# Two attention layers in one kernel: the other layer first, and the output projection in seven Strassen products, half of them between the dense heads

## The chip, the cores and the metric

The kernel runs on one core of a Trainium2 chip. The metric is the device time of one execution in microseconds, shown as the median of several runs. The engines that matter are TensorE (PE, with its weight load PEld), VectorE (DVE), ScalarE (ACT) and GpSimd (POOL). Transfers between DRAM and the core's SBUF are issued from the queues of SP (the sync engine), ACT and POOL. Each engine works through its own queue in order; semaphores hold an instruction until what it needs is there.

## The reference

Two attention layers run on inputs of their own, and their outputs are concatenated. Each has 2048 positions, 1024 features and 32 heads of 32.

```python
def _A_ref(x, wqkv, wo):
    ...
    W, dil = 8, 2
    ...
    idx = pos[:, None] - off[None, :]
    ...
    logits = jnp.einsum("bhsd,bhswd->bhsw", q, kg) * scale
    logits = jnp.where(mask[None, None, :, :], logits, -1e9)
    attn = _softmax(logits, axis=-1)
    o = jnp.einsum("bhsw,bhswd->bhsd", attn, vg)
    return (lambda x, *d: x.transpose(*d))(o, 0, 2, 1, 3).reshape(B, S, D) @ wo

def _B_ref(x, wqkv, wo):
    ...
    mask = (idx[:, None] - idx[None, :] >= 0) & (idx[:, None] - idx[None, :] < W)
    scores = jnp.where(mask[None, None], scores, -1e9)
    p = _softmax(scores, axis=-1)
    o = jnp.einsum("bhqk,bhkd->bhqd", p, v)
    return (lambda x, *d: x.transpose(*d))(o, 0, 2, 1, 3).reshape(B, S, D) @ wo
```

In layer A (the window layer here) each position attends to eight positions, two apart. In layer B (the dense layer here) it attends to the 256 positions that end with itself. Both end with an output projection, a 2048 x 1024 by 1024 x 1024 product.

## The kernel before

The work is cut into eight *units*: four chunks of 512 positions of each layer. `ORDER` puts the four dense units first, then the four window units. A unit has eight *groups* of four heads (128 features). For each group `qk_items` computes q and k: two matrix products, each eight feature blocks (k) of three 128x512 matmuls (L518). There are three matmuls because every operand is kept as a high and a low part: `Stream.parts` casts the loaded fp32 data to fp32r (the high part, L201 on ACT or L204 on DVE, whichever a model of the engines says ends first) and subtracts (the low part, L207 on DVE), and `TERMS` multiplies high by high, high by low and low by high. `v_items` computes v for four or two groups at a time (L583). `o_items(u, n)` computes one 128-row block of a unit's output projection (L645): eight groups' outputs `ot`, also high and low (`finish`, L822 and L826), times eight blocks of `wo`, summed in one PSUM bank, copied out (`copy_out`, L536 or L539) and stored (L662).

All weights and inputs come through one list, `items`, in the order in which they are used. `Stream.load_to` issues a load of 512 KB per item on POOL's queue (L159) into a ring of `NRAW` = 3 raw tiles; `split_to` splits it into the tiles of `wpool` (3 buffers) or `xpool` (`NX`). A raw tile is loaded again only when its last subtraction is done.

The order of the program is written by a loop at the end of the kernel. It keeps a clock for each engine (`Clock`) and takes, at each step, the next thing that is ready from four sequences: a helper one, the second phase of the heads, the first phase, and the matrix products (`gemm`, in the order of `plan`). In `plan` the projections of a unit stand between the q/k products of the next unit (`O_SLOTS`), and those of the last unit at the end, the first four of them with their last feature block held back (`TAIL`).

A dense group: `stack` places q and k, high and low, by DMA on SP's queue into `qst` and `kst` (two buffers, L479, with the previous chunk's last keys from DRAM, L408); first scores (L857), maximum (L862) and sum (L867) for each of 16 tiles; the logarithm goes back into `qst` (L902), and rows of ones in `kst` (L341) let a second score product (L940) come out normalized; ACT takes the exponential (L947), POOL or DVE masks the corners (L926, L929), and a product with v follows (L987). A window group: q and k are rearranged by eight small DMAs (L438) into `seats`, a part of `pbuf`; 64 small products (L711); softmax on DVE and ACT (L719 to L749); the result is spread (L758, L761) into `wide`, which shares its memory with `kst`, and multiplied with v (L774). `clear` zeroes these window buffers (L810, L814, POOL) once the dense heads have let go of them.

## Time and profile before

| | us |
|---|---|
| median of 3 runs | 1830.61 (1827.76 to 1834.19) |
| span of the profiled execution | 1830.6 |
| its own time | 1830.61 |

In the page and the views, busy times are shares of the span; a row of a group shows busy time, the mean duration of one instruction in ns, and the idle time before it with what ended it. In the rows of waits, the engine and the line that waited stand first, then what it waited for, the total in us, the number of times and the longest. In this execution the last dense group ends at about 1030 us and the first window scores start at 1042 us. TensorE's granted clock was 0.999 of full speed.

### The profile page before, as it was taken

The page shows a single profiled execution, that of the slowest core. Times are in us where ns is not written, and L with a number is a line of the kernel's source. Part 1 is how long each engine was busy: PE and PEld are TensorE (multiplying, and loading weights), DVE is VectorE, ACT ScalarE, POOL GpSimd, SP SyncE. Part 2 cuts the span into 40 slices and gives each one's busy share as a digit, 9 for nine tenths or more (in the row PEclk, how much of TensorE's full clock was granted, in tenths as well). Part 3 has the DMA queues.
Part 4 walks back from the last instruction along what each step waited for, and adds up shares of the span by engine and source line. Part 5 has one row for each costly group of instructions (what it writes and reads, how often), then busy time and mean ns, then how long its engine had stood idle before and what let it go on. Part 6 is the DMA issues. An engine that isn't in the chain of part 4 may idle for free.

```text
span 1830.6 us, 38331 instructions
## 1 busy us (share of the span) xinstructions
PE 1807.8 (99%) x14826; PEld 1477.5 (81%) x14826; DVE 1202.9 (66%) x2694; ACT 889.4 (49%) x2254; POOL 394.4 (22%) x926
## 2 busy tenths in 40 slices
...
GB/s 242 121 138 139 176 164 150 170 121 160 164 155 164 136 151 183 125 157 141 141 142 130 110 135 116 152 143 130 119 115 143 133 138 108 162 107 128 127 104 83
DMA packets 109141, 257.43 MB, mean 141 GB/s; under 512 B 14496, under 2 KB 29856, under 8 KB 108960
## 3 DMA queue, kind: packets, MB, share of 16 engines
...
HBM read 164.63 MB, written 23.07 MB: 103 GB/s over the span
## 4 chain that ended last, share of the span: by engine, by line
PE 92%; DVE 4%; DMA 2%; ACT 2%; issue 1%; SPq 0%; ACTq 0%; POOL 0%; DVEq 0%; POOLq 0%
PE g L518 37%; PE g L645 19%; PE g L583 17%; PE s L940 5%; PE s L857 5%; PE o L987 5%; PE s L711 2%; PE o L774 2%; DMA raw<-xs 1%; DVE w L207 1%; DVE s L862 1%; ACT s L867 0%; DMA qst<-nat 0%; DMA pbuf<-nat 0%; DVE x L207 0%
## 5 line engine op out<-in xcount | busy, mean ns | idle before, releaser
L518 PE MATMUL g<-x,w 128*128 128x512 f32 x3072 | 770.2, 394 | 3.8 <-DVE nm L729 2.4
L518 PEld LDWEIGHTS g<-x,w 128*128 128x128 f32 x3072 | 566.3, 189 | 114.2 <-issue 8.3
L583 PE MATMUL g<-w,x 128*128 128x256 f32 (+1 forms) x2304 | 391.9, 320 | 0.9 <-issue 0.7
L207 DVE TENSOR_TENSOR w<-raw,w 128x512 fp32r<-128x512 f32 x516 | 338.6, 698 | 52.0 <-ACT w L201 44.8
L583 PEld LDWEIGHTS g<-w,x 128*128 128x128 f32 x2304 | 332.3, 190 | 29.2 <-DVE w L207 1.8
L645 PE MATMUL g<-ot,w 128*128 128x512 f32 x1416 | 343.6, 393 | 3.7 <-DVE ot L826 1.8
L867 ACT ACTIVATE s<-s,nm 128x384 f32<-128x384 f32 (+2 forms) x512 | 274.3, 536 | 102.1 <-DVE nm L862 101.8
L862 DVE CUSTOM_DVE_ANT_0 s<-s,mask_d 128x384 f32<-128x384 f32 (+2 forms) x512 | 261.5, 553 | 88.2 <-PE s L857 87.5
L645 PEld LDWEIGHTS g<-ot,w 128*128 128x128 f32 x1416 | 262.4, 188 | 59.3 <-DVE ot L826 3.2
L926 POOL TENSOR_SCALAR_AFFINE_SELECT pbuf<-pbuf 128x128 f32<-128x128 f32 (+1 forms) x606 | 219.8, 391 | 325.1 <-ACT pbuf L947 323.8
L947 ACT ACTIVATE pbuf<-s 128x384 f32<-128x384 f32 (+2 forms) x480 | 202.7, 505 | 72.2 <-PE s L940 70.2
L159 POOL DMA_DIRECT2D raw<-wqk x126 | 68.1, 540 | 457.5 <-DVE w L207 356.3
L204 DVE CAST w<-raw 128x1024 fp32r<-128x1024 f32 x205 | 141.7, 691 | 24.8 <-PE g L518 24.0
L940 PEld LDWEIGHTS s<-qst,kst 128*128 128x128 f32 x704 | 113.0, 188 | 41.2 <-ACT s L867 16.3
L857 PE MATMUL s<-kst,qst 96*128 96x384 f32 (+2 forms) x512 | 142.4, 342 | 0.9 <-ACT s L867 0.6
L940 PE MATMUL s<-qst,kst 128*128 128x256 f32 (+2 forms) x704 | 136.5, 302 | 3.5 <-ACT s L867 3.0
L719 DVE TENSOR_TENSOR band<-s,near 128x160 f32<-128x160 f32 x128 | 32.4, 315 | 158.0 <-PE s L711 158.0
L536 ACT COPY ost<-g 128x512 f32<-128x512 f32 x54 | 31.7, 587 | 207.1 <-PE g L645 200.4
L857 PEld LDWEIGHTS s<-kst,qst 96*128 96x128 f32 x512 | 93.4, 189 | 26.2 <-issue 4.7
L826 DVE TENSOR_TENSOR ot<-o,ot 128x512 fp32r<-128x512 f32 x64 | 44.0, 688 | 101.6 <-ACT ot L822 101.4
L867 ACT ACTIVATION_READ_ACCUMULATOR s<-s,nm 128x1 f32 x512 | 105.3, 206 | 0.0
L159 POOL DMA_DIRECT2D raw<-wo x64 | 34.2, 534 | 304.2 <-DVE w L207 260.2
...
## 6 DMA issues: line engine op xcount, KB each, us to landing
raw<-wqk POOLq DMA_DIRECT2D x126, 512.0 KB, 4.3
raw<-wv POOLq DMA_DIRECT2D x72, 512.0 KB, 5.1
raw<-wo POOLq DMA_DIRECT2D x64, 512.0 KB, 4.1
qst<-nat SPq DMA_DIRECT2D x96, 256.0 KB, 5.3
kst<-nat SPq DMA_DIRECT2D x96, 256.0 KB, 5.6
raw<-xs POOLq DMA_DIRECT2D x28, 512.0 KB, 4.6
outs<-ost ACTq DMA_DIRECT2D x56, 256.0 KB, 2.3
...
```

Source lines behind the costliest of these rows:

```text
L159: (self.nc.scalar if early else self.nc.gpsimd).dma_start(raw if len(ap.shape) == 2 else raw.rearrange("p (a b) -> p a b", a=2), ap)
L204: nc.vector.tensor_copy(t[:, 0, :], raw)
L207: nc.vector.tensor_tensor(t[:, 1, c:c + 512], raw[:, c:c + 512], t[:, 0, c:c + 512].bitcast(F32), op=ALU.subtract)
L518: nc.tensor.matmul(h["ps"], h["w"][:, a, k * P:(k + 1) * P], xt[u][k][:, b, :], start=(k == 0 and i == 0), stop=(k == NK - 1 and i == 2))
L583: nc.tensor.matmul(ps, xt[u][kw * g + k][:, a, p0:p0 + P], h["w"][g][:, c, k], start=(first and t == 0 and half == 0), stop=(last and t == 2),
L645: nc.tensor.matmul(h["ps"], w[:, a, c:c + P], ot[u, k][:, b, :], start=(k == 0 and i == 0), stop=(k == NK - 1 and i == 2))
L857: nc.tensor.matmul(ps[:, :n], q[0:96, j, b * P:(b + 1) * P], kk[0:96, j, c0:c1], start=True, stop=True)
L862: nc.vector.tensor_tensor_reduce(ps[:, :n], ps[:, :n], mask[:, cut:full], scale=-1.0, scalar=BIG, op0=ALU.add, op1=ALU.min, accum_out=nm)
L867: nc.scalar.activation(ps[:, :n], ps[:, :n], AF.Exp, bias=nm, scale=-1.0, accum_out=sm)
L926: nc.gpsimd.affine_select(w, w, pattern=[[0, m], [step, n]], compare_op=ALU.is_ge, fill=0.0, base=base, channel_multiplier=chan)
L940: nc.tensor.matmul(ps[:, i * n:(i + 1) * n], kk[:, j, 256 + kb * P:256 + (kb + 1) * P], q[:, j, q0:q0 + n], start=True, stop=True)
L947: nc.scalar.activation(w, ps[:, :pack * n].rearrange("p (j n) -> p j n", j=pack), AF.Exp)
```

## The change

The window layer comes first: `ORDER` starts with units 4 to 7 of the inputs, so the window units are now numbered 0 to 3 in the program and the dense ones 4 to 7. Window buffers are cleared at the start, by DVE; `stacks` makes the dense buffers, with their ones, when the last two window groups have finished.

The output projection is done for a pair of units `v` (1024 positions) as a 2 x 2 block product in seven products for eight (Winograd's form of Strassen). Rows are the pair's two units, the inner dimension is split into groups 0 to 3 and 4 to 7, and the output features in the same way. Each product (`o_items(v, i)`) has four output blocks of four feature blocks of three matmuls: 48. `finish` no longer splits a head's output: ACT copies it, and SP stores it to DRAM (`od`). The sums of the output blocks (`sd`) and of the weight blocks (`td`) are made by `background`, one task at a time: loads on SP's queue, four operations of 128x256 on POOL, one store on SP's queue. For the last pair `last_sum` makes them with DVE. A product's operands are four items of the stream, two of rows and two of weights, each 512 KB from `od`, `sd`, `td` or `wo`; a gate keeps the load of an item back until the modelled clock says that its data has landed. The results of a product are added to SBUF tiles by DVE straight from PSUM (the first of a pair is copied by ACT), and stored when complete.

`O_AT` puts the 14 products of the window layer between the dense layer's groups; the 14 of the dense layer stand at the end of `plan`. In the built program five of these still stand between the last dense heads' work, and the last nine (432 matmuls) have nothing between them. The special order of the last unit's projection (`TAIL`) is gone. The thresholds by which `parts` picks ACT or DVE for a cast are changed, and `xpool` has 13 buffers.

```diff
-NRAW, NP, NO, NS = 3, 768, 10, 4
+NRAW, NP, NS = 3, 768, 4
 ASK = 2
 SIDE = 6
-SIDE_X, SIDE_W = -99, -99
-LIGHT, LIGHT_FROM = 0.5, (4, 1)
+SIDE_X, SIDE_W = 0.0, -0.3
+LIGHT, LIGHT_TO = 0.5, (4, 0)
 MASK_BIAS = 0.2
 ROWS_LATE, KEYS_LATE = 0, 1.2
 SEAT_LATE = 4.0
 VPARTS = ((0,4),(4,2),(6,2))
 V_SLOTS = {0:0,5:1,7:2}
-O_SLOTS = {2: (0, 1), 3: (2, 3), 4: (4, 5), 5: (6, 7)}
+PRODUCTS = (("11", "11"), ("12", "21"), (0, 3), (2, 2), ("22", 1), (3, 0), (1, "22"))
+BG_FROM, BG_REST, BG_SLACK = (120.0, 900.0), 3.0, 2.0
 V0_SLOTS = {1:0,3:1,7:2}
-NX, NST, NN = 9, 1, 3
-TAIL, XAT = 4, 1
+NX, NST, NN = 13, 1, 3
+XAT = 1
 C1, C3, CG, CV = 0.108, 0.2, 0.231, 0.242
 CW = 1.36
-ORDER = (0, 1, 2, 3, 4, 5, 6, 7)
+ORDER = (4, 5, 6, 7, 0, 1, 2, 3)
+O_AT = {(4, 2): 0, (4, 3): 1, (4, 4): 2, (4, 6): 3, (5, 2): 4, (5, 3): 5, (5, 4): 6, (5, 6): 7, (6, 2): 8,
+        (6, 3): 9, (6, 4): 10, (6, 6): 11, (7, 2): 12, (7, 3): 13}
 BANK_LATE = 0.0
 EARLY, WARM = 1.0, 10
...
-            if u and s in O_SLOTS:
-                plan += [("o", u - 1, n) for n in O_SLOTS[s]]
             plan.append(("qk", u, s))
             vs = V_SLOTS if u else V0_SLOTS
             if s in vs:
                 plan.append(("v", u, vs[s]))
+            if (u, s) in O_AT:
+                plan.append(("o", O_AT[u, s] // 7, O_AT[u, s] % 7))
         if u + 1 < U:
             plan.append(("x", u + 1))
-    plan += [("o", U - 1, n) for n in range(NG)]
+    plan += [("o", v, i) for v in range(U // 2) for i in range(7) if 7 * v + i not in O_AT.values()]
...
+    od = [dram.tile([P, NG, S], F32, name=f"od{u}") for u in range(U)]
+    sd = [dram.tile([P, 4, 4, S], F32, name=f"sd{v}") for v in range(U // 2)]
+    td = [dram.tile([P, 4, 4, S], F32, name=f"td{ly}") for ly in range(2)]
...
+    def landed(key, *which):
+        return lambda: all(done[key].get(w, ck.now + 1) <= ck.now for w in which)
+    def o_parts(v, i):
+        ly = units[2 * v][0]
+        for a, b in PRODUCTS[i:i + 1]:
+            for j in range(2):
+                key = ("o", v, i, "s", j)
+                if isinstance(a, str):
+                    u, c = 2 * v + int(a[0]) - 1, 4 * (int(a[1]) - 1) + 2 * j
+                    item(key, "xw", od[u][:, c:c + 2, :])
+                    gates[where[key]] = landed("ot", u * NG + c, u * NG + c + 1)
+                else:
+                    item(key, "xw", sd[v][:, a, 2 * j:2 * j + 2, :])
+                    gates[where[key]] = landed("s", *[(v, k, c) for k in (2 * j, 2 * j + 1) for c in (0, 256)])
+            for j in range(2):
+                key = ("o", v, i, "t", j)
+                if isinstance(b, str):
+                    n, c = 4 * (int(b[1]) - 1) + 2 * j, S * (int(b[0]) - 1)
+                    item(key, "w", wo[ly, n:n + 2, :, c:c + S].rearrange("n p c -> p n c"))
+                else:
+                    item(key, "w", td[ly][:, b, 2 * j:2 * j + 2, :])
+                    gates[where[key]] = landed("t", *[(ly, n, c) for n in (2 * j, 2 * j + 1) for c in (0, 256)])
...
+            gate = self.gates.get(self.loaded)
+            if gate and not gate():
+                return
...
-        bias = EARLY if side else LIGHT if self.split >= self.light else SIDE_W if n > S else SIDE_X
+        bias = EARLY if side else LIGHT if self.split < self.light else SIDE_W if n > S else SIDE_X
...
+            w, x = held["o", v, i, "t", n // 2][0], held["o", v, i, "s", k // 2][0][k % 2]
+            c = S * (n % 2) + P * k
+            for t, (a, b) in enumerate(TERMS):
+                nc.tensor.matmul(h["ps"], w[:, a, c:c + P], x[:, b, :], start=(k == 0 and t == 0),
+                                 stop=(k == 3 and t == 2))
+            if k == 1:
+                at = where["o", v, i, "t", 1]
+                if [kind for kind, _ in st.items[at + 1:at + n + 1]].count("w") < 3:
+                    st.split_to(min(at + n + 1, len(st.items)))
+        def after(i, n, k):
+            if k < 3:
+                return
+            ps, bank = h["ps"], h["b"]
+            def add(dst, src):
+                nc.vector.tensor_tensor(dst, ps, src, op=ALU.add)
+                return ck.use("dve", 0.61, ck.now + ck.SEM)
+            def new(name):
+                return sums.tile([P, S], F32, tag=f"{name}{n}", name=name)
+            def store(r, c, tile, e):
+                def go():
+                    nc.scalar.dma_start(outs[ORDER[2 * v + r], 4 * c + n], tile)
+                    ck.load("store", e)
+                ck.defer(e, go)
+            if i == 0:
+                h["a", n] = new("a")
+                nc.scalar.copy(h["a", n], ps)
+                e = ck.use("act", 0.485, ck.now + ck.SEM)
+            elif i == 1:
+                o = stp.tile([P, S], F32, tag="ost", name="ost")
+                e = add(o, h["a", n])
+                store(0, 0, o, e)
+            elif i == 2:
+                e = add(h["a", n], h["a", n])
+            elif i == 3:
+                h["c", n] = new("c")
+                e = add(h["c", n], h["a", n])
+            elif i == 4:
+                o = stp.tile([P, S], F32, tag="ost", name="ost")
+                e = add(o, h["c", n])
+                store(1, 0, o, e)
+            elif i == 5:
+                e = add(h["c", n], h["c", n])
+                store(1, 1, h["c", n], e)
+                e = add(h["a", n], h["a", n])
+            else:
+                e = add(h["a", n], h["a", n])
+                store(0, 1, h["a", n], e)
+            rg.give(bank, e)
+        for n in range(4):
+            for k in range(4):
+                    at = (i, n, k)
+                    out.append((lambda at=at: ready(*at), lambda at=at: run(*at), 3 * CG, lambda at=at: after(*at)))
+        return out
+    def background():
+        if bg["busy"] or not bg["tasks"]:
+            return
+        bg["busy"] = True
+        loads, ops, dst, key, who = bg["tasks"].pop(0)
+        t = bgp.tile([P, 4, S // 2], F32, tag="bg", name="bg")
+        for c, ap in loads:
+            nc.sync.dma_start(t[:, c:c + 2, :], ap)
+            e = ck.copy("load", ck.now)
+        def add():
+            for to, x, y, op in ops:
+                nc.gpsimd.tensor_tensor(t[:, to, :], t[:, x, :], t[:, y, :], op=op)
+                e = ck.use("pool", 0.62, ck.now)
+            ck.defer(e, finish)
+        def finish():
+            nc.sync.dma_start(dst, t)
+            e = ck.copy("load", ck.now)
+            def end():
+                done[key][who] = ck.now
+                bg["busy"] = False
+                st.load_to(st.wanted)
+                background()
+            ck.defer(e + BG_REST, end)
+        ck.defer(e + BG_SLACK, add)
+    def task(*what):
+        bg["tasks"].append(what)
+        background()
+    def weight_sums(ly):
+        for n in range(4):
+            for c in range(0, S, 256):
+                task([(2 * i, wo[ly, n + 4 * i].rearrange("p (a b) -> p a b", a=2)[:, :, c:c + 256]) for i in range(2)],
+                     ((0, 2, 0, ALU.subtract), (2, 3, 2, ALU.subtract), (3, 3, 0, ALU.subtract), (1, 1, 3, ALU.subtract)),
+                     td[ly][:, :, n, c:c + 256], "t", (ly, n, c))
+    def output_sums(v, k):
+        for c in range(0, S, 256):
+            task([(2 * r, od[2 * v + r][:, k::4, c:c + 256]) for r in range(2)],
+                 ((3, 2, 3, ALU.add), (2, 0, 2, ALU.subtract), (0, 3, 0, ALU.subtract), (1, 1, 0, ALU.subtract)),
+                 sd[v][:, :, k, c:c + 256], "s", (v, k, c))
...
+    def last_sum(v):
+        k = tail[0]
+        t = [natp.tile([P, 2 * S + 16], F32R, tag="nat", name="nat").bitcast(F32) for _ in range(2)]
+        t = [t[i // 2][:, i % 2 * S:i % 2 * S + S] for i in range(4)]
+        for i in (0, 2, 1, 3):
+            nc.sync.dma_start(t[i], od[2 * v + i // 2][:, k + 4 * (i % 2), :])
+            e = ck.copy("half", ck.now)
+        def go():
+            for to, x, y, op in ((3, 2, 3, ALU.add), (2, 0, 2, ALU.subtract), (0, 3, 0, ALU.subtract),
+                                 (1, 1, 0, ALU.subtract)):
+                nc.vector.tensor_tensor(t[to], t[x], t[y], op=op)
+                e2 = ck.use("dve", 0.61, e, port=True)
+            def put():
+                for i in (2, 0, 3, 1):
+                    nc.sync.dma_start(sd[v][:, i, k, :], t[i])
+                    e3 = ck.copy("half", e2)
+                def end():
+                    for c in range(0, S, 256):
+                        done["s"][v, k, c] = ck.now
+                    st.load_to(st.wanted)
+                    tail.pop(0)
+                    if tail:
+                        last_sum(v)
+                ck.defer(e3 + 1.0, end)
+            ck.defer(e2, put)
+        ck.defer(e, go)
+    for i in range(2):
+        ck.defer(BG_FROM[i], lambda ly=units[i * U // 2][0]: weight_sums(ly))
...
+    def stacks(buf):
+        qst[buf] = stackp.tile([P, 4, S], F32R, tag=f"q{buf}", name=f"qst{buf}")
+        kst[buf] = stackp.tile([P, 4, 256 + S], F32R, tag=f"k{buf}", name=f"kst{buf}")
+        zero = cst["mask_d"][96:P, None, P:2 * P].to_broadcast([32, 24, P])
+        nc.scalar.activation(kst[buf][96:P, :, :].rearrange("p j (a s) -> p (j a) s", s=P), zero, AF.Identity,
+                             bias=1.0, scale=1.0)
+        ck.use("act", 2.7, ck.now)
     def clear(buf):
 
         band[buf] = stackp.tile([P, 4 * S], F32, tag=f"q{buf}", name="band")
-        nc.gpsimd.memset(band[buf][:, :1024], 0.0)
-        ck.use("pool", 1.2, ck.now)
+        nc.vector.memset(band[buf][:, :1024], 0.0)
+        ck.use("dve", 0.6, ck.now)
         k = stackp.tile([P, 4, 256 + S], F32, tag=f"k{buf}", name="wide")
         wide[buf] = k.rearrange("p j s -> p (j s)")[:, :4 * 544].rearrange("p (j c) -> p j c", j=4)
-        nc.gpsimd.memset(wide[buf], 0.0)
-        done["clear"][buf] = ck.use("pool", 2.5, ck.now)
+        nc.vector.memset(wide[buf], 0.0)
+        done["clear"][buf] = ck.use("dve", 1.2, ck.now)
 
     def finish(u, s, h):
         hg = u * NG + s
         done["o"][hg] = ck.now
-        o = opool.tile([P, 2, S], F32R, tag="ot", name="ot")
-        ot[u, s] = o
-        nc.scalar.copy(o[:, 0, :], h["o"])
-        r = ck.use("act", 0.485, ck.now + ck.SEM)
-        def low():
-            nc.vector.tensor_tensor(o[:, 1, :], h["o"], o[:, 0, :].bitcast(F32), op=ALU.subtract)
-            e = ck.use("dve", 0.61, r)
-            ro.give(0, e)
-            done["ot"][hg] = e
-        ck.defer(r, low)
+        if nw - 2 <= hg < nw:
+            stacks(hg % 2)
+            free_keys(hg)
+        o = otp.tile([P, S], F32, tag="ot", name="ot")
+        nc.scalar.copy(o, h["o"])
+        e = ck.use("act", 0.485, ck.now + ck.SEM)
+        ro.give(0, e)
+        def store():
+            nc.sync.dma_start(od[u][:, s, :], o)
+            e2 = ck.copy("store", e)
+            def end():
+                done["ot"][hg] = ck.now
+                st.load_to(st.wanted)
+                if s >= 4 and u % 2:
+                    (last_sums if u == U - 1 else output_sums)(u // 2, s - 4)
+            ck.defer(e2 + 1.0, end)
+        ck.defer(e, store)
 
...
-    n = TAIL
-    tail = [gemm[len(gemm) - NG * NK + i * NK:len(gemm) - NG * NK + (i + 1) * NK] for i in range(NG)]
-    del gemm[len(gemm) - NG * NK:]
-    for i in range(n):
-        gemm += tail[i][:NK - 1]
-    for i in range(n):
-        gemm += tail[i][NK - 1:]
-    for i in range(n, NG):
-        gemm += tail[i]
```

154 lines of the change are left out of this document (72 added, 82 removed).

## The prediction

> **What bounds the kernel now.** I read the busy times first, then the chain that ended last.
>
> ```profile
> PE 1807.8 (99%) x14826; PEld 1477.5 (81%) x14826; DVE 1202.9 (66%) x2694; ACT 889.4 (49%) x2254; POOL 394.4 (22%) x926
> ...
> PE 92%; DVE 4%; DMA 2%; ACT 2%; issue 1%; SPq 0%; ACTq 0%; POOL 0%; DVEq 0%; POOLq 0%
> PE g L518 37%; PE g L645 19%; PE g L583 17%; PE s L940 5%; PE s L857 5%; PE o L987 5%; PE s L711 2%; PE o L774 2%; DMA raw<-xs 1%; DVE w L207 1%; DVE s L862 1%; ACT s L867 0%; DMA qst<-nat 0%; DMA pbuf<-nat 0%; DVE x L207 0%
> ```
>
> TensorE is busy 99% of the span, and 92% of the chain is its own work; the output projection (L645) holds 19%. A busy matmul row can hide small gaps, so I looked next at what TensorE waits for: first the dense layer's stretch without its start (20 to 1040 us), then the window layer's.
>
> ```profile
> PE s L896 <- DVE hl L888: 3.6, 4, 2.0
> PE s L940 <- ACT s L867: 3.0, 4, 1.1
> PE g L645 <- ACT ot L822: 0.7, 1, 0.7
> PE g L645 <- DVE ot L826: 0.7, 3, 0.2
> ...
> PE g L518 <- DVE nm L729: 2.4, 1, 2.4
> PE g L645 <- DVE band L719: 1.2, 1, 1.2
> PE g L645 <- DVE ot L826: 1.1, 1, 1.1
> ```
>
> With the smaller rows (three and two), that is 9.1 us in the first stretch and 6.4 us in the second. So an output matmul that goes away shortens the kernel by its own pitch, as long as the work that now feeds TensorE keeps up.
>
> The stages differ. The windows give PE, PEld, DVE, ACT and POOL busy time, then the clock, the DMA share and GB/s.
>
> ```profile
> 0.00:1040.00 1040.00, 1027.43 (x6176) 827.70 (x6177) 766.13 (x1960) 597.33 (x1710) 318.98 (x789) 1.00 0.55 152
> 1040.00:1780.00 740.00, 734.59 (x8384) 613.14 (x8383) 418.60 (x705) 280.82 (x524) 73.28 (x133) 1.00 0.42 129
> ...
> 100.00:200.00 100.00, 96.43 (x600) 78.26 (x599) 77.61 (x220) 55.71 (x173) 32.55 (x77) 1.00 0.49 136
> 200.00:260.00 60.00, 58.42 (x327) 44.94 (x328) 47.52 (x129) 37.99 (x116) 16.57 (x43) 1.00 0.67 176
> ...
> 1114.70:1227.90 113.20, 113.20 (x1249) 95.84 (x1241) 71.09 (x121) 47.26 (x87) 13.68 (x24) 1.00 0.45 134
> ```
>
> VectorE is 74% busy in the dense half and 57% in the window half. The last row is window heads with no output matmul between them, up to its end: TensorE has no gap there, at 63% VectorE. The two rows above it are dense heads with none (the first output matmul comes at 260 us): at 78% VectorE, TensorE lost 3.57 + 1.58 = 5.2 us of 160, or 3.2%.
>
> **The change, part by part.**
>
> *Matmuls removed.* The output projection issues 1536 matmuls now (rows of 1416, 96 and 24); in the built program it is 28 products of 48, or 1344. The pitch comes from the last run of them:
>
> ```profile
> 1804.96 21.92 PE L645 MATMUL g<-ot,x 128*128 128x512 f32 x96
> ...
> L645 PE MATMUL g<-ot,w 128*128 128x512 f32 x1416 | 343.6, 393 | 3.7 <-DVE ot L826 1.8 <-DVE band L719 1.2 <-ACT ot L822 0.7
> L645 PE MATMUL g<-ot,x 128*128 128x512 f32 x96 | 21.9, 389 | 0.0
> ```
>
> (21.92 - 0.39) / 95 = 0.2266 us. 192 x 0.2266 = **43.5 us less**, all on the bounding engine. A product is 10.88 us.
>
> *Splits and additions.* Prices are these groups:
>
> ```profile
> L207 DVE TENSOR_TENSOR w<-raw,w 128x512 fp32r<-128x512 f32 x516 | 338.6, 698 | 52.0 <-ACT w L201 44.8
> L204 DVE CAST w<-raw 128x1024 fp32r<-128x1024 f32 x205 | 141.7, 691 | 24.8 <-PE g L518 24.0 <-PE g L583 0.6
> L201 ACT CAST w<-raw 128x1024 fp32r<-128x1024 f32 x52 | 54.1, 1047 | 10.9 <-PE g L583 6.4 <-ACT ost L536 2.7 <-DVE band L731 0.7
> L201 ACT CAST x<-raw 128x512 fp32r<-128x512 f32 x31 | 17.8, 618 | 22.7 <-DMA raw<-xs 19.9 <-DVE x L204 2.6
> L536 ACT COPY ost<-g 128x512 f32<-128x512 f32 x54 | 31.7, 587 | 207.1 <-PE g L645 200.4 <-PE s L940 5.5 <-DMA kst<-nat 1.2
> ```
>
> The stream holds 112 items for the products where it held 64 for the projection. By the counts of the built program VectorE gets 32 more low-half subtractions (96 for the added items, less the 64 of `ot`), 112 additions onto product banks and 16 sums near the end. Two such operations back to back take 1.29 us (a row quoted below), so 160 x 0.645 = +103 us. It loses 69 whole-width casts (-48 us) and 7 bank copies (-5 us): +50 us, so 1253 us, 70% of the span. ScalarE gets 66 casts of 1024 columns and 104 of 512 (69 + 64 us), and 43 bank copies fewer (-25 us): 56%. Neither becomes the bound on average. In the dense half, VectorE's instructions between the first dense score and the last dense row, priced by the page's means, go from 869 to 910 us, +5%; TensorE's time there also grows: 1040 - 24 x 24 x 0.2266 + 19 products (14 of the window layer, five of 14 dense ones) x 10.88 = 1116 us, less some 26 us of start-up that stays with the first layer, so about 1090. The share stays 74%. Cost: nothing while TensorE's products cover it.
>
> *Sums on GpSimd.* 40 tasks with four 128x256 operations each, half of them in the dense half. No two-input operation of GpSimd stands in the trace; the nearest rows are its one-input selects:
>
> ```profile
> L926 POOL TENSOR_SCALAR_AFFINE_SELECT pbuf<-pbuf 128x128 f32<-128x128 f32 x440 | 141.1, 351 | 166.3 <-ACT pbuf L947 165.8
> L926 POOL TENSOR_SCALAR_AFFINE_SELECT pbuf<-pbuf 128x256 f32<-128x256 f32 x166 | 79.9, 495 | 158.8 <-ACT pbuf L947 157.9
> ...
> L204 DVE CAST x<-raw x39: 385/420/1367, 185.4 to 1810.7; 128x512 fp32r<-128x512 f32 x39
> ```
>
> Bounds 0.35 and 0.99 us (twice the 256-column row); I take 0.7, since the input is 256 columns twice. 160 x 0.7 = 112 us on an engine that idles 78%. The cast that took 1367 ns beside a median of 420 shows VectorE held up once. If every sum in the dense half held VectorE for its whole length, that is 80 x 0.7 = 56 us, and (766 x 1.05 + 56) / 1090 = 79%, where the 160 us above lost 3.2%. I take 1 us; bounds 0 and 26 us (3.2% of 1090 is 35, less the 9 us lost today).
>
> [...]
>
> *Traffic and queues.* All bytes moved, the landing times (the second `raw<-wv` from 200 to 260 us alone, the second `outs<-ost` from 1440 to 1640 us) and the fastest slice:
>
> ```profile
> DMA packets 109141, 257.43 MB, mean 141 GB/s; under 512 B 14496, under 2 KB 29856, under 8 KB 108960
> ...
> raw<-wqk POOLq DMA_DIRECT2D x126, 512.0 KB, 4.3
> raw<-wv POOLq DMA_DIRECT2D x72, 512.0 KB, 5.1
> ...
> raw<-wv POOLq DMA_DIRECT2D x3, 512.0 KB, 7.1
> ...
> outs<-ost ACTq DMA_DIRECT2D x56, 256.0 KB, 2.3
> ...
> outs<-ost ACTq DMA_DIRECT2D x8, 256.0 KB, 3.5
> ...
> 5.00:10.00 5.00, 3.78 (x10) 1.72 (x9) 3.33 (x5) 2.93 (x6) 4.27 (x10) 1.00 0.99 347
> ```
>
> Added: 48 items (25 MB), 64 stores of a head's output (17), loads and stores of the 40 tasks (42), the last sums (8): 92 MB on 257, so 196 GB/s. In the dense half I count 223 MB in 1090 us, 205 GB/s against 152, a share of 0.74 by the ratio. In the last 98 us (432 matmuls, nine products, with nothing between) 36 items, 24 stores and one set of sums are 27 MB, 279 GB/s under the 347 once reached.
>
> What sets the feed there is the ring of three raw tiles: a product takes four items in 10.88 us, 2.72 each, so a tile must come round in 8.16 us.
>
> ```profile
> 1795.99 1.29 DVE L207 TENSOR_TENSOR x<-raw,x 128x512 fp32r<-128x512 f32 x2
> 1797.58 0.53 POOL L159 DMA_DIRECT2D raw<-wo  x1 [5.56 <-DVE x L207]
> ```
>
> 0.3 us from the last subtraction to the next issue, a landing of 4.3, a cast of 1.05, 1.29 for the subtractions and some 0.3 of hand-overs make 7.2. At 5.1 it is 8.0; at 7.1 (the short window at 0.67 DMA share, 200 to 260 us) it is 10.0, or 13.3 us a product. Bounds for the nine: 0 and 22 us; nearest to the first two rows, I take 3. In the dense half attention stands between the products, and I take 2.5 more of wait there (bounds 0 and 26, shared with the sums). On SP's queue the stores of `ot` and the tasks stand ahead of q/k placements: the same bounds hold.
>
> A new wait: in products 1 and 4 of a pair every block is added into `ost`, which has one buffer. An addition (0.69) waits for the store of the block before (2.3, or 3.5 in the busier stretch) and so comes every 3.2 to 4.4 us with hand-overs, against 2.72 for a block's matmuls. Three banks cover the delay itself; but behind the waiting addition on VectorE stand the splits of the next product, which TensorE needs at once. By the last block that is 1.4 to 5 us. Two such products lie in the last nine: bounds 0 and 10, and I take 1.5, since the splits have about a microsecond to spare at the ring's 7.2. The other six are stretched by attention.
>
> *Start, switch, end.* The window buffers are cleared by VectorE at the start:
>
> ```profile
> 0.98 0.48 DVE L1052 MEMSET qst<- 128x512 f32 x1 [0.98 <-PEq L1119]
> ...
> 5.45 0.87 DVE L207 TENSOR_TENSOR x<-raw,x 128x512 fp32r<-128x512 f32 x1 [3.98 <-ACT x L201]
> ...
> L341 ACT ACTIVATE kst<-mask_d 32x3072 fp32r<-32x3072 f32 x2 | 5.4, 2766 | 0.0
> ```
>
> 6400 columns at 0.48/512 us are 6.0 us, to 7.5, so the first subtraction comes up to 2 us late; few matmuls are ready by then: +0.3. The two 2.77 us fills of ones move to the switch; 57 V matmuls (12.9 us) stand there in TensorE's order: nothing, 2.8 us without them. The last addition replaces a copy: +0.1.
>
> The sum, against the profiled execution's 1830.6 us (the median of the three runs): 1830.6 - 43.5 + 1 + 3 + 2.5 + 1.5 + 0.4 = **1795.5 us**, 1795 in round numbers.
>
> **The rivals.**
>
> *The tail is fed too slowly.* Landings near 6.5 us in the last nine products make a ring of 9.4 us, 12.6 a product: +15 us; with the other costs of the sum 1808. For it: 0.8 of the fastest rate asked for. Against: the program splits the four items of a product while the one before it runs, so a single late tile is absorbed.
>
> *VectorE is held up in the dense half* by sums and splits: the 26 us above, 1830.6 - 43.5 + 26 = 1813. For it: the 160 us at 78%. Against: there TensorE had no projection to fill in; after the change it has 19 products.
>
> *Slower: late loads everywhere.* GpSimd's queue issues the items and also holds the sums, which wait for their own loads; an item behind them goes out late. If each of the 28 products ran at the 13.3 us of a 7.1 us landing, the change costs 28 x 2.4 = 67 us: 1854. It decides from 43.5 / 28 = 1.55 us a product, a landing of 6.5. For it: that landing occurred. Against: only three loads show it, and in the dense half attention stretches a product beyond 13 us, so the ring has time.
>
> *The saving is eaten exactly*, or the chain moves off TensorE: 1826 to 1836.
>
> **How the numbers follow.** Forecast 0.64, tail 0.14, dense half 0.11, eaten 0.04, slower 0.07. Faster by over 0.3% (5.5 us, about what a measurement can tell): 0.64 + 0.14 + 0.11 = 0.89; within 0.04; slower 0.07. Low end: no cost, and the waits of L645 in the rows (3.7 us) gone too, 1783. High end: the dense rival with the 3 us of the tail, 1816.
>
> **What would show it.** Right: 1344 output matmuls at 0.227 us; TensorE's waits under 25 us in all; no gap above 1 us in the last 98 us; raw landings near 4.5 us; GpSimd's sums at 0.35 to 0.99 us. Wrong: raw landings at 6 us or more with TensorE waiting for VectorE's splits in the tail; VectorE's casts far above 0.69 us while GpSimd sums run; TensorE waiting on dense scores after late SP placements.

## The result, and the profile after

| | median us | lowest to highest | runs | ratio to before, 95% interval |
|---|---|---|---|---|
| before | 1830.84 | 1827.76 to 1834.19 | 4 | |
| after | 1908.96 | 1904.02 to 1912.78 | 4 | 1.0422 [1.0401, 1.0444] |

The changed kernel is 78 us slower; the forecast was 1795, with a range of 1783 to 1816. The profiled execution of after took 1912.78 us (span 1911.1). Its page gives the busy times and the chain that ended last:

```profile
PE 1821.8 (95%) x14634; PEld 1466.3 (77%) x14634; DVE 1286.9 (67%) x2795; ACT 988.6 (52%) x2383; POOL 562.8 (29%) x1115
...
PE 57%; DVE 8%; DMA 8%; ACT 3%; issue 3%; POOL 1%; SPq 0%; DVEq 0%; ACTq 0%; POOLq 0%
PE g L557 23%; PE g L625 11%; PE g L697 9%; PE s L1048 4%; DMA outs<-ost 4%; PE o L1176 4%; PE s L1131 4%; DVE w L217 2%; ACT s L1058 1%; DVE s L1053 1%; DVE qst L1093 1%; PE o L951 1%; PE s L890 1%; DMA raw<-xs 1%; DVE x L217 1%
```

The 192 matmuls are gone (14826 to 14634), yet TensorE is busy 14 us longer. It fell from 99% to 95% of the span, and from 92% to 57% of the chain. In its place stand VectorE and transfers, the store of `ost` first among them with 4%. No engine took over as the bound: VectorE is at 67%. What grew is waiting, and it is spread out. The groups in question:

```profile
L697 PE MATMUL g<-x,w 128*128 128x512 f32 x1344 | 341.3, 399 | 6.7 <-DVE w L217 3.1
L217 DVE TENSOR_TENSOR w<-raw,w 128x512 fp32r<-128x512 f32 x510 | 351.7, 731 | 57.8 <-ACT w L211 52.5
L769 POOL TENSOR_TENSOR bg<-bg 128x256 f32<-128x256 f32 x160 | 135.9, 850 | 76.1 <-DMA bg<-od 20.5 <-DMA pbuf<-nat 20.2 <-DMA bg<-wo 19.8
```

TensorE was idle for 22.8 us of its 1830.6 before, and for 89.3 us of 1911.1 after. The output matmuls (L697) themselves lost only 6.7 us to idle time right before them. The waits of VectorE (first row) and of TensorE (the others) name what the rest waited for; the columns are the total in us, the times, and the longest:

```profile
DVE ost L710 <- DMA outs<-ost: 61.9, 20, 8.7
```

```profile
PE s L1048 <- ACT s L1058: 17.7, 13, 4.3
PE s L1087 <- DVE hl L1079: 9.3, 6, 2.4
...
PE g L625 <- issue: 4.2, 1, 4.2
...
PE s L1048 <- DMA bg<-wo: 3.9, 1, 3.9
```

VectorE stood for 61.9 us in the addition into the single `ost` buffer. The largest of TensorE's own waits are those for the dense layer's softmax (L1048, L1087). "issue" means that the profile names nothing that was waited for. Of the 82.7 us of pauses that TensorE's timeline shows, 47.9 lie in the dense half, 28.7 in the window half (before 670 us) and 6.1 at the end: the victims are mostly heads, not output products.

The transfers are as forecast in bytes, and the item loads (the `raw` rows) land in 4.5 to 5.5 us, near the 4.1 to 5.1 of before. The store of `ost` takes 3.7 where the two rows of before had 2.3 and 3.5:

```profile
DMA packets 172764, 349.77 MB, mean 183 GB/s; under 512 B 18720, under 2 KB 75040, under 8 KB 172576
...
raw<-wqk POOLq DMA_DIRECT2D x126, 512.0 KB, 4.8
...
raw<-xs POOLq DMA_DIRECT2D x28, 512.0 KB, 5.5
...
outs<-ost ACTq DMA_DIRECT2D x32, 256.0 KB, 3.7
```

*Where the waits turn into time.* First the `ost` episode in the timeline of after, 763 to 785 us (start, duration, engine and line, operation, and in brackets the idle time before with what ended it):

```profile
768.01 0.68 DVE L710 TENSOR_TENSOR ost<-g,a 128x512 f32<-128x512 f32 x1
...
773.43 0.69 DVE L710 TENSOR_TENSOR ost<-g,a 128x512 f32<-128x512 f32 x1 [1.80 <-DMA outs<-ost]
...
777.87 0.53 POOL L167 DMA_DIRECT2D raw<-td  x1 [5.18 <-DVE x L217]
...
781.85 0.69 DVE L710 TENSOR_TENSOR ost<-g,a 128x512 f32<-128x512 f32 x1 [4.28 <-DMA outs<-ost]
782.57 0.37 ACTq L718 DMA_DIRECT2D outs<-ost  x1
782.99 0.22 ACT L1071 ACTIVATE ln<-sm 128x16 f32<-128x16 f32 x1 [6.41 <-DVE ost L710]
...
783.97 0.22 PE L1087 MATMUL s<-ident,hl 128*32 128x128 f32 x1 [2.40 <-DVE hl L1079]
```

Product 1 of a pair, inside a dense head. The third and fourth additions wait for the store of the block before. While the fourth one waits, VectorE does nothing for 4.28 us, ScalarE waits 6.41 us to take the logarithm, and TensorE waits 2.40 us for what follows from it. ScalarE waits because the store of `ost` is issued from its own queue (782.57), ahead of the logarithm, and cannot go out before the addition is done. The rows of the tile `ost` show who else stood behind these additions on ScalarE (total in us, times), 33.6 us in ten places:

```profile
  ACT w L211: 13.8, 5
  ACT x L211: 13.4, 4
  ACT ln L1071: 6.4, 1
```

The addition needed nobody's hurry; what stood behind it in VectorE's queue, and behind its store in ScalarE's, did.

Second, GpSimd's queue in the window half, 316 to 330 us of the same timeline:

```profile
316.12 0.53 POOL L167 DMA_DIRECT2D raw<-xs  x1 [13.37 <-ACT x L211]
316.66 3.87 POOL L769 TENSOR_TENSOR bg<-bg 128x256 f32<-128x256 f32 x4
...
320.47 1.09 POOL L167 DMA_DIRECT2D raw<-xs  x2
...
325.77 1.14 ACT L211 CAST x<-raw 128x512 fp32r<-128x512 f32 x2 [4.34 <-DMA raw<-xs]
...
329.87 1.14 ACT L211 CAST x<-raw 128x512 fp32r<-128x512 f32 x2 [2.32 <-DMA raw<-xs]
329.89 1.18 PE L625 MATMUL g<-w,x 128*128 128x256 f32 x7 [4.23 <-issue]
```

Four sums in a row hold GpSimd for 3.87 us, and the two loads of x behind them go out at 320.47. ScalarE then waits for each load in turn.

TensorE stands for 4.23 us in the same stretch, but not for these columns: the v products of a unit read the x columns that its q and k products have used already, and the loads are for the next unit. The profile names nothing that it waited for. The trace does have a transfer of instructions, 16 KB on the queue q8, from 327.46 to 328.40 us, and TensorE goes on 1.5 us later. Each of the six pauses marked "issue" up to 600 us, 10.9 us together, ends 1.3 to 1.6 us after such a transfer, so TensorE was probably waiting for its own program. In the runs below the pause at this place is 4.0 us with fills in place of the additions (e13), 1.2 without the additions (e4) and 0.3 without any sums (e3), but also 0.8 in e14, which makes every sum in another order. What delays the transfer is not shown.

Third, what a gap costs beyond its own length. The windows below are of 1 us each; the third column from the end is TensorE's granted clock, the first number after the width is PE's busy time. The first rows are around a gap that ends at 501.11 us, the last three around one that ends at 375.33:

```profile
500.00:501.00 1.00, 0.00 (x0) 0.00 (x0) 0.93 (x3) 1.00 (x2) 0.00 (x0) 1.00 0.81 66
501.00:502.00 1.00, 0.89 (x2) 0.46 (x2) 0.96 (x2) 0.06 (x1) 0.00 (x0) 0.59 0.86 319
...
507.00:508.00 1.00, 1.00 (x7) 0.35 (x9) 1.00 (x2) 0.30 (x1) 0.31 (x1) 0.50 0.76 299
508.00:509.00 1.00, 1.00 (x33) 0.80 (x33) 0.93 (x3) 0.00 (x0) 0.41 (x1) 0.99 0.04 8
...
374.00:375.00 1.00, 0.00 (x0) 0.00 (x0) 0.96 (x2) 0.93 (x3) 0.57 (x1) 1.00 1.01 349
375.00:376.00 1.00, 0.67 (x20) 0.46 (x24) 1.00 (x3) 0.97 (x3) 0.00 (x0) 1.00 1.12 214
376.00:377.00 1.00, 0.95 (x17) 0.47 (x18) 0.96 (x3) 0.41 (x2) 0.53 (x1) 1.00 0.57 209
```

After the first gap (1.62 us) the clock is at half until 508; after the second (2.08 us) it stays whole. Over after, the sum of (1 - clock) in windows of 2 us is 42.7 us, in 19 stretches, against 2.0 us in before. The gaps that the timeline of TensorE shows add up to 82.7 us, against 18.5. So visible waiting and its clock make (82.7 - 18.5) + (42.7 - 2.0) = 105 us. To be explained are the 80.5 us between the two spans and the 43.5 us that should have gone, 124 us; the other 19 us are not located. They lie inside rows that count as busy, since TensorE's idle time as a whole grew by no more than 66.5 us. (Both sums are rough: a pause inside a lowered stretch counts in each.)

### The profile page after: what moved, and what is told of

Read it like the earlier page. It is cut to its first block, busy times and chain, and to the rows that moved or that the text cites. A ratio compares the mean times of both kernels' runs of the same rounds, so it can differ in the third digit from the quotient of the medians.

```text
span 1911.1 us, 39058 instructions
## 1 busy us (share of the span) xinstructions
PE 1821.8 (95%) x14634; PEld 1466.3 (77%) x14634; DVE 1286.9 (67%) x2795; ACT 988.6 (52%) x2383; POOL 562.8 (29%) x1115
## 2 busy tenths in 40 slices
DMA packets 172764, 349.77 MB, mean 183 GB/s; under 512 B 18720, under 2 KB 75040, under 8 KB 172576
## 4 chain that ended last, share of the span: by engine, by line
PE 57%; DVE 8%; DMA 8%; ACT 3%; issue 3%; POOL 1%; SPq 0%; DVEq 0%; ACTq 0%; POOLq 0%
PE g L557 23%; PE g L625 11%; PE g L697 9%; PE s L1048 4%; DMA outs<-ost 4%; PE o L1176 4%; PE s L1131 4%; DVE w L217 2%; ACT s L1058 1%; DVE s L1053 1%; DVE qst L1093 1%; PE o L951 1%; PE s L890 1%; DMA raw<-xs 1%; DVE x L217 1%
## 5 line engine op out<-in xcount | busy, mean ns | idle before, releaser
L557 PE MATMUL g<-x,w 128*128 128x512 f32 x3072 | 778.1, 401 | 17.0 <-ACT w L211 3.8
L557 PEld LDWEIGHTS g<-x,w 128*128 128x128 f32 x3072 | 579.3, 193 | 140.1 <-issue 9.6
L217 DVE TENSOR_TENSOR w<-raw,w 128x512 fp32r<-128x512 f32 x510 | 351.7, 731 | 57.8 <-ACT w L211 52.5
L697 PE MATMUL g<-x,w 128*128 128x512 f32 x1344 | 341.3, 399 | 6.7 <-DVE w L217 3.1
L697 PEld LDWEIGHTS g<-x,w 128*128 128x128 f32 x1344 | 251.7, 191 | 59.8 <-DVE w L217 7.2
L1048 PE MATMUL s<-kst,qst 96*128 96x384 f32 (+2 forms) x512 | 152.0, 355 | 30.2 <-ACT s L1058 17.7
L769 POOL TENSOR_TENSOR bg<-bg 128x256 f32<-128x256 f32 x160 | 135.9, 850 | 76.1 <-DMA bg<-od 20.5
L211 ACT CAST w<-raw 128x1024 fp32r<-128x1024 f32 (+1 forms) x120 | 124.4, 1042 | 61.3 <-DVE ost L710 13.8
L1131 PE MATMUL s<-qst,kst 128*128 128x256 f32 (+2 forms) x704 | 141.4, 309 | 6.6 <-ACT pbuf L1138 2.2
L1048 PEld LDWEIGHTS s<-kst,qst 96*128 96x128 f32 x512 | 94.7, 192 | 64.6 <-ACT s L1058 29.7
L214 DVE CAST w<-raw 128x1024 fp32r<-128x1024 f32 x136 | 97.3, 715 | 56.7 <-PE g L557 41.2
L211 ACT CAST x<-raw 128x512 fp32r<-128x512 f32 x135 | 78.4, 622 | 105.1 <-DMA raw<-xs 61.2
L217 DVE TENSOR_TENSOR x<-raw,x 128x512 fp32r<-128x512 f32 x172 | 117.8, 721 | 21.5 <-ACT x L211 19.8
```

What stands on the lines that cost most here:

```text
L211: nc.scalar.copy(t[:, 0, :], raw)
L217: nc.vector.tensor_tensor(t[:, 1, c:c + 512], raw[:, c:c + 512], t[:, 0, c:c + 512].bitcast(F32), op=ALU.subtract)
L557: nc.tensor.matmul(h["ps"], h["w"][:, a, k * P:(k + 1) * P], xt[u][k][:, b, :], start=(k == 0 and i == 0), stop=(k == NK - 1 and i == 2))
L697: nc.tensor.matmul(h["ps"], w[:, a, c:c + P], x[:, b, :], start=(k == 0 and t == 0), stop=(k == 3 and t == 2))
L769: nc.gpsimd.tensor_tensor(t[:, to, :], t[:, x, :], t[:, y, :], op=op)
L1048: nc.tensor.matmul(ps[:, :n], qst[buf][0:96, j, b * P:(b + 1) * P], kst[buf][0:96, j, c0:c1], start=True, stop=True)
```

## The experiments

Each kernel below is one edit, or a few, on after; times are medians, ratios are to before on the same chip. "Gaps" is TensorE's visible waiting in the profiled execution, "clock" the time lost to a lowered clock, both read as above. Some kernels leave out work that the result needs (e3, e4, e7, e11, e12, e13, e15 and e16); they are here for their time alone.

### The single store buffer

e1_ost3: three `ost` buffers; the room comes from one x buffer. e2_nx12: the x buffer alone, as a control.

```diff
-NX, NST, NN = 13, 1, 3
+NX, NST, NN = 12, 3, 3
```

> The changed kernel with three `ost` buffers for one (and 12 x buffers for 13, to make room). Theory 1 (the additions of products 1 and 4 wait for the store of the block before, and what stands behind them on VectorE keeps TensorE waiting until its clock is halved): the 62 us that VectorE waits on `outs<-ost` fall under 10 us, about ten of the 18 stretches at half clock go, and the time falls by 30 to 50 us from 1909, to 1860 to 1880. Rival (the sums' transfers and the GpSimd additions set the loss): under 10 us less, 1900 or more. Third (both halves lose by many small waits): 10 to 20 us less.

> The changed kernel with 12 x buffers for 13 and still one `ost` buffer: the control to the run with three. If the x buffers do not matter, within 5 us of 1909 under every theory.

e1: 1874.7 us, 1.0225 [1.0183, 1.0267]. e2: 1904.0, 1.0385 [1.0349, 1.0421]. So the extra buffers are worth 29 us (e2 less e1), the x buffer some 5 at most, which the interval of e2 does not tell from nothing. The first theory's range (1860 to 1880) held. Gaps went from 82.7 to 59.9 us and clock from 42.7 to 23.9, 41.6 us together; the two profiled executions are 40.7 us apart. VectorE no longer waits for the store, and ScalarE's waits for these additions fell from 33.6 to 1.2 us. More buffers free both queues at once, and no run parts the two. The last nine products now run without a stop worth naming; TensorE's timeline of e1:

```profile
1766.39 23.57 PE L697 MATMUL g<-x,w 128*128 128x512 f32 x98
1790.21 76.46 PE L697 MATMUL g<-x,w 128*128 128x512 f32 x334 [0.26 <-DVE w L217]
```

432 matmuls in 100.3 us, where 432 x 0.2266 = 97.9. A ring of three raw tiles feeds the products after all.

### The sums

e3_nosums takes away all sums, GpSimd's and the last ones; the products read plain blocks. e4_noadds keeps every transfer of the 40 tasks and drops only the additions. e13_poolwrite puts a fill in the place of each addition: about as long (987 ns against 850), but it reads nothing.

```diff
 e3, at the head of weight_sums(), in finish() and in o_parts():
+        return
-                if s >= 4 and u % 2:
+                if False:
+            a, b = a if isinstance(a, str) else "22", b if isinstance(b, str) else "11"
 e4, in add():
-                nc.gpsimd.tensor_tensor(t[:, to, :], t[:, x, :], t[:, y, :], op=op)
 e13, in add():
-                nc.gpsimd.tensor_tensor(t[:, to, :], t[:, x, :], t[:, y, :], op=op)
+                nc.gpsimd.memset(t, 0.0)
```

> The changed kernel without any sums of blocks: no loads, additions or stores of the 40 tasks and no last sums; the products read plain blocks of the heads' outputs and of the weights in place of sums. One `ost` buffer stays. Theory 1: the dense half keeps its stalls at products 1 and 4; only what the sums hold up goes, 10 to 25 us, most of it in the window half (the late x tiles near 330, 500 and 668 us): 1885 to 1900. Rival (the sums set the loss): 50 us or more less, under 1860.

> The changed kernel with the 40 tasks' loads and stores but without their four additions on GpSimd (the last pair's sums on VectorE stay). If the additions hold up the item loads behind them on GpSimd's queue (850 ns each in the trace, where the sum had 700), this gives most of what leaving out all sums gives. If the transfers on SP's queue hold up the q and k placements, little: within 5 us of 1909.

> The changed kernel; each of the four additions of a background task is a GpSimd memset of 128x1024, which keeps GpSimd busy about as long (0.94 us in the trace of before, against 0.85) but reads nothing. The sums are left out by it; the transfers stay. If the additions cost what they do by holding up VectorE, whose operations read two tiles: near the run without additions, 1875 to 1885. If they cost it by keeping the item loads and the masks behind them waiting on GpSimd's queue: near 1909, 1900 or more.

e3: 1867.3, 1.0184 [1.014, 1.0228]; e4: 1878.7, 1.0246 [1.0217, 1.0276]; e13: 1906.4, 1.0403 [1.0383, 1.0424]. All sums are worth 42 us, the additions on GpSimd alone 30; transfers and the last sums share the other 12. e3 falls between the two ranges expected for it (1885 to 1900, or under 1860); e4 gave most of what e3 gave, as expected if the additions hold up what stands behind them. And the fills, which read no SBUF, cost what the additions cost (1906 against 1909):

```profile
L769 POOL MEMSET bg<- 128x1024 f32 x160 | 157.9, 987 | 64.8 <-DMA pbuf<-nat 25.4 <-DMA bg<-wo 19.5 <-DMA bg<-od 13.0
```

So it is GpSimd's time in its queue, and not the reading, that costs; as the fills are 16% longer, a few us for the reading are not excluded. Before this row, 64.8 us of waiting for transfers stand at the head of that queue, where everything behind waits too. VectorE's subtraction (L217) took 731 ns in after, 708 in e13 and 706 in e4 (the row of 510): the neighbour's reads cost it 25 ns a time, 17 us over its 682 instructions, on an engine that is not full. The 25 ns do not carry the time here.

Then the order in GpSimd's queue. e6_price makes the order-writing model count an addition at its measured spacing. e14_ost3_price joins that to e1. e17_ost3_spread, from e14, releases the four additions of a task one at a time, 2 us after the modelled end of the last; e18_ost3_sync, from e14, issues item loads on SP's queue instead.

```diff
 e6 and e14, in add():
-                e = ck.use("pool", 0.62, ck.now)
+                e = ck.use("pool", 1.0, ck.now)
 e17, in background():
-        def add():
-            for to, x, y, op in ops:
-                nc.gpsimd.tensor_tensor(t[:, to, :], t[:, x, :], t[:, y, :], op=op)
-                e = ck.use("pool", 0.62, ck.now)
-            ck.defer(e, finish)
+        def add(i=0):
+            to, x, y, op = ops[i]
+            nc.gpsimd.tensor_tensor(t[:, to, :], t[:, x, :], t[:, y, :], op=op)
+            e = ck.use("pool", 1.0, ck.now)
+            ck.defer(e + 2.0 if i < 3 else e, (lambda: add(i + 1)) if i < 3 else finish)
 e18, in load_to():
-            (self.nc.scalar if early else self.nc.gpsimd).dma_start(raw if len(ap.shape) == 2 else raw.rearrange("p (a b) -> p a b", a=2), ap)
-            self.raw[self.loaded] = raw, (self.ck.load if early else self.ck.fetch)("load", self.ck.now)
+            (self.nc.scalar if early else self.nc.sync).dma_start(raw if len(ap.shape) == 2 else raw.rearrange("p (a b) -> p a b", a=2), ap)
+            self.raw[self.loaded] = raw, (self.ck.load if early else self.ck.copy)("load", self.ck.now)
```

> The changed kernel; only the price of a GpSimd addition in the model that writes the order is 1.0 us in place of 0.62 (the trace has 850 ns each, 1.01 apart). The same work in an order that leaves room for it. Theory (the additions cost what they do because the order takes them for shorter: the SP queue's store and the item loads behind them stand too early): 10 to 25 us less, 1885 to 1900. [...]

> Three `ost` buffers and the price of 1.0 us for a GpSimd addition, all the reference's work done, thresholds as in the changed kernel. The two alone gave 34 and 17 us. If they are separate: 1858. If both act through the same waits of VectorE: 1865 to 1875.

> The kernel with three ost buffers, twelve x buffers and the price of 1.0 us for a GpSimd addition (1868.6 us), with one edit more: the four additions of a task are not issued in one burst but one by one, each 2 us after the model's end of the one before, so that item loads can go between them in GpSimd's queue. Theory (the sums cost about 30 us because four additions, some 4 us with their waits, stand in front of item loads in GpSimd's queue): a load then waits for one addition of about 1 us at most, 1845 to 1858 us. Rival (the cost is the additions' later end, the background traffic and VectorE's lack of slack, not the burst): 1865 us or more; the tasks also end 6 us later each, so the operands of some products land later.

> The same kernel (three ost buffers, twelve x buffers, price 1.0; 1868.6 us) with the item loads issued on SP's queue in place of GpSimd's; additions and the rest unchanged. Theory (what hurts is that item loads stand behind the additions in GpSimd's queue): without that neighbour the time falls to 1835 to 1855 us, if SP's own waits do no harm. Rival: SP's queue holds the placements of q and k and the tasks' loads and stores, each waiting for its producer, and a raw load behind them goes out late as well: 1870 us or more, with TensorE waiting for splits (L217) behind raw loads issued from SP.

e6: 1892.4, 1.0329 [1.0299, 1.0358], 17 us better and inside its theory's range. e14: 1868.6, 1.0201 [1.0184, 1.0219]; joined to the buffers the price is worth only 6, so the two overlap. e17: 1847.9, 1.0088 [1.0071, 1.0105], 21 us better than e14 with every sum still made: the theory's range held, the rival's did not. e18: 1859.3, 1.0158 [1.0124, 1.0192], 9 us better, between the two ranges; what SP's queue costs in its place is not shown. GpSimd's timeline of e17 shows what changed:

```profile
302.74 0.57 POOL L167 DMA_DIRECT2D raw<-wqk  x1 [0.85 <-DVE w L217]
303.33 0.75 POOL L769 TENSOR_TENSOR bg<-bg 128x256 f32<-128x256 f32 x1
306.26 0.57 POOL L167 DMA_DIRECT2D raw<-xs  x1 [2.19 <-DVE w L217]
306.86 0.75 POOL L769 TENSOR_TENSOR bg<-bg 128x256 f32<-128x256 f32 x1
```

Loads go out between additions. Gaps fell from 62.3 to 51.1 us and clock from 21.1 to 15.9, which is 16 of the 21 us. e17 is the best version found that does all the work; it is still slower than before.

### VectorE's load

e5_castdve sets the thresholds for casts back to before's: 182 of the stream's casts move from ScalarE to VectorE, 73 stay on ScalarE. e8_ost3_price_castdve is that with e14; e10_ost3_price_castact pushes more casts to ScalarE, with e14. e15_ost3_nolow, from e1, leaves out the low parts of the products' operands: 224 fewer subtractions, the same number of matmuls.

```diff
 e5 and e8:
-SIDE_X, SIDE_W = 0.0, -0.3
+SIDE_X, SIDE_W = -99, -99
 e10:
+SIDE_X, SIDE_W = 0.8, 0.5
 e15, in parts() for items of products, and in o_items():
+        if plain:
+            return r
-                nc.tensor.matmul(h["ps"], w[:, a, c:c + P], x[:, b, :], start=(k == 0 and t == 0),
+                nc.tensor.matmul(h["ps"], w[:, 0, c:c + P], x[:, 0, :], start=(k == 0 and t == 0),
```

> The changed kernel with the thresholds for the casts as before the change (every cast of the stream on VectorE except at the start and in the window half, where the light threshold stays). Theory (casts on ScalarE stand ahead of the exponentials and wait there for their loads, 61 us of ScalarE waiting for x loads): the waits of dense score matmuls for ScalarE's exponential, 17.7 us, halve and the time falls by 10 to 20 us from 1909. Rival (VectorE is the fuller engine and the casts are better off on ScalarE): slower, 1915 or more.

> Three `ost` buffers, the price of 1.0 us for a GpSimd addition, and the casts' thresholds as before, all the reference's work done. If the three causes are separate and of the sizes expected (34, 15, 15): 1845. If only the buffers matter: 1870 to 1880.

> Three `ost` buffers, 1.0 us as the price of a GpSimd addition, and thresholds that give ScalarE more of the casts, all the reference's work done. Moving casts to VectorE cost 44 us. Theory (VectorE is what holds the dense half): 1835 to 1855, below the 1858 that the first two should give together. Rival (ScalarE's casts delay its exponentials as much): 1860 or more.

> Three `ost` buffers, all sums done, but no low parts of the products' operands (224 subtractions fewer on VectorE; high by high three times). Without sums that gave 33 us. If the causes are separate: 1875 - 33 = 1842. If a full VectorE is the root and the sums cost because it is full: 1815 to 1830.

e5: 1953.4, 1.0661 [1.063, 1.0692]. The theory said faster and it was 44 us slower; the range of the rival, that VectorE is the fuller engine, held. e8: 1901.1, 1.0376 [1.0346, 1.0406], 33 us above e14, a like loss; it missed both of its ranges, which took e5 for a gain. e10: 1867.2, 1.0192 [1.0144, 1.0241], nothing against e14, though VectorE was busy 34 us less (1251.1 against 1285.4): the theory's 1835 to 1855 was missed, the rival's 1860 or more held. e15: 1848.4, 1.0087 [1.0067, 1.0107], 26 us below e1, nearer to the 1842 expected of separate causes than to the 1815 to 1830 of a full VectorE as the root. Leaving out the low parts does a second thing, which no run parts from VectorE's load: a raw tile is free after its cast, without the 1.29 us of its two subtractions, so the next load can go out sooner. The thresholds that the change brought were needed. The page of e5 shows how little of it an average tells:

```profile
PE 1839.5 (94%) x14634; PEld 1473.7 (76%) x14634; DVE 1385.8 (71%) x2974; ACT 858.8 (44%) x2198; POOL 579.7 (30%) x1121
```

99 us more on VectorE, at 71% in all, cost TensorE 21.4 us more of gaps (104.1) and 15.3 more of clock (58.0), 37 of the 40 us between the two profiled executions.

### Joined, down to the forecast

e7_ost3_nosums joins e1 and e3. e12_nosums_noout is e7 without the stores of the heads' outputs (rows read from the inputs). e11_nosums_nolow is e7 without low parts. e16_nosums_noout_nolow is all three. e9_ost3_end, from e1, puts all products at the end of the plan; in the built program 270 of their matmuls (5.6 products) still run among the last dense heads, where e1 has 912 (19 products).

```diff
 e12, in o_parts() and finish():
-                    item(key, "xw", od[u][:, c:c + 2, :])
+                    item(key, "xw", xs[u][:, c:c + 2, :])
-            nc.sync.dma_start(od[u][:, s, :], o)
 e9:
+O_AT = {}
```

> Three `ost` buffers and no sums of blocks (the products read plain blocks of the heads' outputs and of the weights; 12 x buffers). Alone the two gave 34 and 42 us. If they are separate causes: 1909 - 76 = 1833, so still no faster than before, and some 45 us of the predicted 43.5 are lost to a third cause. If a third of each is shared: 1845 to 1860.

> The run without sums and with three `ost` buffers (1834), and also without the 64 stores of the heads' outputs on SP's queue; the products read their rows from the input instead. Theory (VectorE's load is the rest): within 5 us of 1834. Rival (the stores stand ahead of q and k placements on SP's queue; one gap of 3.1 us was put down to them): 10 to 20 us less.

> The run without sums and with three `ost` buffers (1834), and also without the low parts of the products' operands: VectorE loses 224 subtractions (some 145 us), and the products multiply high by high three times, so TensorE's work is the same. Theory (what is left of the loss is VectorE's load by the products): 1795 to 1810, near 1787. Rival (what is left comes from queues of transfers or from the order of the layers): within 10 us of 1834.

> Three `ost` buffers, no sums, no stores of the heads' outputs (the products read their rows from the input) and no low parts of the products' operands. What is left of the change is the order of the layers, 192 matmuls fewer, four items for each product and the additions. If nothing else costs: 1790 to 1800, the 1787 of the sum without costs. If the order of the layers costs by itself: 1800 or more.

> Three `ost` buffers, and all 28 products at the end of the plan: none between the dense heads, all the reference's work done. Theory (the products' splits and additions crowd VectorE in the dense half, which was full there already): the dense half loses less, the end pays its ring, and the time falls by 10 to 30 us from the 1875 with three buffers. Rival (dense heads without a matrix product to fill their waits lose more than the products cost): 1880 or more.

| kernel | us | step | gaps | clock | ratio to before |
|---|---|---|---|---|---|
| after | 1909.0 | | 82.7 | 42.7 | 1.0422 [1.0401, 1.0444] |
| one x buffer less (e2) | 1904.0 | -5 | | | 1.0385 [1.0349, 1.0421] |
| three `ost` buffers (e1) | 1874.7 | -29 | 59.9 | 23.9 | 1.0225 [1.0183, 1.0267] |
| no sums (e7) | 1834.4 | -40 | 45.5 | 24.3 | 1.0012 [0.9998, 1.0025] |
| no low parts (e11) | 1801.1 | -33 | 25.9 | 8.6 | 0.9832 [0.9803, 0.986] |
| no output stores (e16) | 1799.3 | -2 | 26.4 | 8.6 | 0.9819 [0.9799, 0.9839] |

e12 is 1828.1, 0.9976 [0.9962, 0.9991], 6 us below e7, between the two ranges expected (within 5 us of 1834, or 10 to 20 less). e7 and e11 lie where they were expected if the causes are separate (1833, and 1795 to 1810), e16 just inside its 1790 to 1800. Each step was taken on top of the one before; the sums cost 42 us alone and 40 here, the low parts 26 with the sums and 33 without, so the causes add up nearly. With all three taken away the kernel stands at 1799, 4 us above the sum of the prediction: the 43.5 us of matmuls did leave, and everything priced near nothing took them back. TensorE's largest waits in e11 (its lines lie some five further down than in after: L1054 are the first scores) are:

```profile
PE s L1054 <- ACT s L1064: 5.5, 4, 3.0
PE o L957 <- issue: 4.9, 3, 2.5
PE g L562 <- DVE x L220: 3.3, 1, 3.3
```

e9 missed: 1908.2, 1.0416 [1.0385, 1.0448], 33 us worse than e1. Its rival's range (1880 or more) held. The windows of e9 over the dense heads and over the end, then that of e1 over its dense heads:

```profile
670.00:1700.00 1030.00, 990.19 (x5816) 771.12 (x5815) 720.71 (x1853) 636.10 (x1765) 379.93 (x888) 0.97 0.65 186
1700.00:1907.00 207.00, 201.34 (x886) 165.61 (x884) 146.44 (x233) 73.80 (x102) 39.37 (x68) 1.00 0.76 232
```

```profile
670.00:1766.00 1096.00, 1062.54 (x6261) 844.91 (x6265) 823.70 (x2033) 678.93 (x1815) 404.93 (x868) 0.99 0.67 195
```

At the end of e9, 912 matmuls run at full clock in one row of 207.61 us, (207.61 - 0.39) / 911 = 0.2275 apart. In the stretch of its dense heads TensorE is idle 39.8 us against 33.5 in e1, though the stretch is shorter and its last 45 us are products alone, and the lowered clock (windows of 2 us) costs 32 us there against 12: 27 of the 33 us. A head that has no product to fill its waits pays in the clock as well.

## Why the prediction was wrong

*The matmuls removed: right.* 192 are gone, and the pitch in a long unbroken run is 0.2275 (e9) against 0.2266. The forecast of the traffic was right (257 + 92 = 349 MB; 349.77), so was VectorE's share in the dense half: 74% forecast, 73% measured by a window from 680 to 1797 us (812.15 us of 1117). Over the whole run VectorE was busy 1286.9 us, 34 more than the 1253 forecast.

*The wait on `ost`: the mechanism right, its place and size wrong.* The prediction priced it at 1.5 us with bounds 0 and 10, for the two products of the tail, and dropped the rest in one clause: "The other six are stretched by attention." They are; but the stall is not TensorE's matmuls waiting for a bank. It is VectorE's queue and, since the store is issued there, ScalarE's, and in the dense half these two hold the softmax. The additions waited 61.9 us in 20 places, and the extra buffers gave back 29 us. The step before it in the same paragraph had named the right question, what stands behind the waiting addition, and answered it only where splits stood there. The store's landing was taken as 2.3 to 3.5; it was 3.7, up to 9.5.

*The sums on GpSimd: the duration inside its bounds, the term wrong.* 850 ns lies between 0.35 and 0.99. The 1 us taken for the stage was for VectorE held up by the sums (bounds 0 to 26, the upper one with every sum holding it for its whole length). In after the 43 subtractions (L217) that overlap an addition took 1.08 us in the mean, the other 639 0.71: 16 us of VectorE's time where the upper bound took 56 in the dense half alone, and 25 ns a time over all (731 against 706 in e4). What cost 30 us (42 with the transfers and the last sums) is what the slower rival names: sums wait for their own loads in the queue that issues the items, and an item behind them goes out late. The price that the prediction gave that rival hung on a landing of 6.5 us; landings stayed at 4.5 to 5.5. An item was late because it was issued late, not because it landed slowly, so the point from which that rival "decides" was put on the wrong number. The stall of VectorE that stood for this term was misread as well: casts of 1.37 us occur three times in before (439.00, 695.50 and 951.94 us), not once, each beside a row of six GpSimd selects (2.80 to 2.81 us).

*VectorE's load: "Cost: nothing while TensorE's products cover it."* This failed in the size of the term too. The share was right, and 33 us (26 with the sums) came back when 224 of the subtractions left. The reading, argued and not shown wait by wait, is that a mean of 73% hides queues of a few microseconds each time that an item, a row maximum and an addition come together, and that TensorE pays in the dense heads' waits for the softmax. Some of the 33 us may belong to loads that go out sooner. The row that spoke of it was there: 5.2 us lost of 160, at 78%. It was read as what happens without a product in the stage, and the 26 us made from it went into a rival.

*The clock: no term at all.* In before the clock fell only at the start (0.66 from 10 to 15 us) and in the last 0.5 us, and gaps of 2.0 and 2.4 us passed without it. After, with 82.7 us of gaps, 43 us went to the clock: about half as much again.

*The start: small, but off.* The clears on VectorE were put at 0.3 us; by 20 us, TensorE had issued 40 matmuls in after against 51 in before: eleven at 0.2266 are 2.5 us. That the clears are the cause was not tried.

*The tail: right in the feed.* With more `ost` buffers 432 matmuls took 100.3 us; the 3 us taken is met, and the rival of a slow feed is refuted. In after the same 432 took 110.5 us (1796.96 to 1907.41), in e2, also with one `ost` buffer, 107.3: `ost` cost the tail 7 us.

*The sum.* 1795.5 with 29 for 1.5, 40 for 1, 33 for nothing and 2.5 for 0.3 is 1897; the 5 us of x buffers and 2 of stores make 1904. The remaining 5 us are within what these differences carry. The steps were measured one on top of the other and so add up of themselves; what tests the account is the last kernel, 1799 against 1795.5. Even the slowest rival, at 1854, stopped 55 us short of the result. The sums still cost 13 us when spread (1847.9 in e17 against 1834.4 without them), about the 12 that their transfers and the last sums cost in e3 and e4. What is left open is how the 33 us that went with the low parts divide between item splits, softmax and sooner loads, how the `ost` wait divides between VectorE's queue and ScalarE's, what delays the transfers of instructions behind the waits marked "issue", and where the 19 us inside busy rows come from.

*What would show it right.* Of the signs listed, 1344 matmuls, the landings and the sums' duration came out; the waits of TensorE did not stay under 25 us (82.7), and there were three gaps above 1 us in the last 110 us (1.94, 1.21 and 1.35).
